# Attention on transposed scores, big-row loads, and a hand-written order of MM1, MM2 and attention

## The chip, the cores and the metric

The kernel runs on one core of one Trainium2 chip. The metric is device time in microseconds of one execution; three runs of the kernel before gave 509.43, 510.44 and 511.20 us, median 510.44. The engines are TensorE (PE for matmuls, PEld for weight loads in the profile), VectorE (DVE), ScalarE (ACT), GpSimd (POOL) and SyncE (SP), each with an instruction stream of its own.

## What is computed

The inputs q, k, v have the shape (batch 8, heads 8, sequence 576, head size 64), in f32. Heads 0 to 3 attend only to the last 32 positions, heads 4 to 7 only to earlier positions that are equal modulo 32:

```python
scores = scale * np.matmul(q, k.transpose(0, 1, 3, 2))
rel = pos[:, None] - pos[None, :]
mask_local = (rel >= 0) & (rel < stride)
mask_strided = (rel >= 0) & (pos[None, :] % stride == pos[:, None] % stride)
...
attn = np.exp(scores)
attn = attn / (np.sum(attn, axis=-1, keepdims=True) + 1e-09)
return np.matmul(attn, v).astype(np.float32)
```

The result, laid out as x of 4608 tokens by 512, goes through two dense layers: h = x @ w_in (512 by 2048), r = max(h, 0), out = (r * r) @ w_out (2048 by 512). The output is f32.

## The kernel before

Heads are worked on in pairs, so that a unit (a pair of one batch entry) has 128 rows of head size. The batch has 32 units, two local and two strided ones per batch entry. `attn_local_pair` loads q and k as 64 partitions by 9 rows and transposes each with nine 64-column transposes (L175), copies them out of the bank (L177), and takes the scores of six blocks of 96 queries by 128 keys (L201). `softmax_T` takes the exponential (L126), multiplies each block by a mask and sums its rows in the same instruction (L135), takes the reciprocal (L140) and builds a diagonal matrix of the reciprocals (L148). A matmul with that diagonal transposes and normalises the weights (L220), ScalarE copies them (L227), a matmul with v follows (L233), and VectorE writes the result into xt, the transposed x (L238). `attn_strided_pair` does the same on rows that are regrouped by residue modulo 32; each group of 7 residues is a block of 126, the last one of 72 (L264 to L336), and v comes in ten loads (L256).

xt has 4608 columns, cut into nine chunks of 512. For a chunk, MM1 has 16 output blocks of four matmuls each (L349), a relu on ScalarE (L353) and a square on VectorE (L354); MM2 has four row blocks of 16 matmuls each (L363), a copy on ScalarE (L367) and a store by SP (L368).

The order that the code is written in is attention by unit, with quarters of MM1 and whole MM2s between units (`drain_moe`). The framework then orders the instructions of each engine by a schedule of its own, and gives out the buffers. PSUM has eight banks: one for transposes, two for scores, two for the weights, one for the output of attention, one for MM1 (psh) and one for MM2 (psy). All loads go through POOL's queue, which also converts f32 to bf16.

## Time and profile before

| | |
|---|---|
| timed runs, median | 510.44 us |
| span of the profiled execution | 512.0 us |
| PE busy | 414.4 us, 81% |
| DVE busy | 281.4 us, 55% |
| POOL busy | 253.7 us, 50% |
| ACT busy | 196.8 us, 38% |
| packets on POOL's queue | 152896 |

The profiled execution's own time is its span: the profile shows nothing around it, and it lies 1.6 us above the median of the timed runs. Busy time of PE counts a matmul from its start to a modelled end, which lies after the start of the next one, so the price of a matmul is read from the distance of starts, and a wait shorter than that tail does not show as idle. An idle time names the engine and line that released it.

### The profile page before, as it was taken

The page shows a single profiled execution, that of the slowest core. Times are in us where ns is not written, and L with a number is a line of the kernel's source. Part 1 is how long each engine was busy: PE and PEld are TensorE (multiplying, and loading weights), DVE is VectorE, ACT ScalarE, POOL GpSimd, SP SyncE. Part 2 cuts the span into 40 slices and gives each one's busy share as a digit, 9 for nine tenths or more (in the row PEclk, how much of TensorE's full clock was granted, in tenths as well). Part 3 has the DMA queues.
Part 4 walks back from the last instruction along what each step waited for, and adds up shares of the span by engine and source line. Part 5 has one row for each costly group of instructions (what it writes and reads, how often), then busy time and mean ns, then how long its engine had stood idle before and what let it go on. Part 6 is the DMA issues. An engine that isn't in the chain of part 4 may idle for free.

```text
span 512.0 us, 8132 instructions
## 1 busy us (share of the span) xinstructions
PE 414.4 (81%) x2784; PEld 198.7 (39%) x2784; DVE 281.4 (55%) x1232; ACT 196.8 (38%) x437; POOL 253.7 (50%) x392
## 2 busy tenths in 40 slices
PE   1344489897999799879987998799889987779775
...
GB/s 36 197 139 98 69 59 63 91 88 64 41 31 103 70 39 54 92 108 49 41 66 69 31 35 66 70 31 32 57 42 1 2 42 42 0 1 61 20 22 61
DMA packets 158121, 29.23 MB, mean 57 GB/s; under 512 B 150912, under 2 KB 152960, under 8 KB 158080
## 3 DMA queue, kind: packets, MB, share of 16 engines
q0 software_dynamic: 152896, 19.27, 53.8%
...
## 4 chain that ended last, share of the span: by engine, by line
PE 65%; POOL 11%; DVE 9%; ACT 7%; issue 4%; DMA 3%; POOLq 0%; ACTq 0%
PE psh L349 29%; PE psy L363 22%; DVE xt L336 7%; ACT r_sb L353 6%; POOL svwb L256 3%; PE po L233 3%; PE po L322 2%; DMA w_in_b<-in_moe_w_in_dram 2%; PE psc L201 2%; PE pat L302 2%; PE pat L220 2%; PE ptr L175 1%; POOL w_out_b L114 1%; DVE e_m L135 1%; POOL vt L186 1%
## 5 line engine op out<-in xcount | busy, mean ns | idle before, releaser
L349 PE MATMUL psh<-xt,w_in_b 128*128 128x512 bf16 x576 | 171.8, 411 | 22.5 <-ACT r_sb L353 16.9
L363 PE MATMUL psy<-w_out_b,g_sb 128*128 128x512 bf16 x576 | 156.0, 389 | 3.2 <-ACT y_sb L367 2.3
L353 ACT ACTIVATE r_sb<-psh 128x512 bf16<-128x512 f32 x144 | 86.0, 597 | 148.0 <-PE psh L349 146.8
L256 POOL DMA_DIRECT2D svwb<-in_v_dram x160 | 99.9, 744 | 22.4 <-PE pat L302 15.2
L354 DVE TENSOR_TENSOR g_sb<-r_sb 128x512 bf16<-128x512 bf16 x144 | 60.3, 418 | 82.5 <-ACT r_sb L353 82.3
L349 PEld LDWEIGHTS <-w_in_b 128*128 128x128 bf16 x576 | 53.5, 102 | 78.9 <-issue 41.8
L363 PEld LDWEIGHTS <-g_sb 128*128 128x128 bf16 x576 | 55.7, 99 | 67.4 <-issue 9.0
L336 DVE CAST xt<-po 128x504 bf16<-128x504 f32 (+1 forms) x32 | 45.0, 1408 | 49.7 <-PE po L322 49.2
L126 ACT ACTIVATE e_sb<-psc 96x512 bf16<-96x512 f32 (+2 forms) x96 | 44.8, 517 | 37.3 <-PE psc L201 23.1
L367 ACT COPY y_sb<-psy 128x512 f32<-128x512 f32 x36 | 21.1, 586 | 94.3 <-PE psy L363 76.5
L148 DVE TENSOR_TENSOR diag<-ident,rinv 96x384 bf16<-96x384 bf16 (+2 forms) x96 | 50.4, 525 | 0.3
L135 DVE CUSTOM_DVE_ANT_0 e_m<-e_sb,mask_loc_g 96x128 bf16<-96x128 bf16 x192 | 46.4, 277 | 4.6 <-ACT e_sb L126 4.2
L135 DVE CUSTOM_DVE_ANT_0 e_m<-e_sb,mask_str 126x126 bf16<-126x126 bf16 (+1 forms) x160 | 36.1, 271 | 21.4 <-ACT e_sb L131 11.9
L322 PE MATMUL po<-sat_sb,svwb 126*64 126x126 bf16 (+1 forms) x160 | 16.4, 234 | 33.5 <-DVE xt L336 12.4
L168 POOL DMA_DIRECT2D kb<-in_k_dram x32 | 25.9, 812 | 25.3 <-PE ptr L175 18.5
L249 POOL DMA_DIRECT2D kb<-in_k_dram x32 | 27.4, 862 | 22.2 <-PE ptr L264 22.1
L166 POOL DMA_DIRECT2D qb<-in_q_dram x32 | 26.7, 850 | 19.4 <-PE ptr L175 17.7
L247 POOL DMA_DIRECT2D qb<-in_q_dram x32 | 27.5, 866 | 16.8 <-PE ptr L264 16.2
L186 POOL DMA_DIRECT2D vt<-in_v_dram x32 | 32.5, 1016 | 0.4 <-issue 0.2
L227 ACT CAST at_sb<-pat 128x384 bf16<-128x384 f32 (+1 forms) x64 | 25.0, 396 | 11.8 <-PE pat L220 11.2
L135 DVE DVE_READ_ACCUMULATOR2_ANT ssum<- 96x1 f32 (+2 forms) x352 | 28.5, 81 | 0.0
L322 PEld LDWEIGHTS <-svwb 126*64 126x64 bf16 (+1 forms) x160 | 10.0, 115 | 44.8 <-issue 17.9
...
## 6 DMA issues: line engine op xcount, KB each, us to landing
...
w_in_b<-in_moe_w_in_dram POOLq DMA_DIRECT2D x4, 512.0 KB, 8.9
...
svwb<-in_v_dram POOLq DMA_DIRECT2D x128, 15.8 KB, 2.3
...
```

Of the source, the lines that this page charges most:

```text
L126: nc.scalar.activation(e_sb[:, 0:gn, :], ps_sc[:, 0:gn, :], AF.Exp, scale=scale)
L135: nc.vector.tensor_tensor_reduce(out=e_m[0:w, t, 0:mask3[t].shape[-1]], in0=e_sb[0:w, t, 0:mask3[t].shape[-1]], in1=mask3[t], scale=1.0, s ...
L148: nc.vector.tensor_tensor(diag4[0:w, 0:gn, 0:w], id_b, rinv[0:w, 0:gn, :].to_broadcast([w, gn, w]), op=ALU.mult)
L186: nc.gpsimd.dma_start(out=vt[:, 1:6, hh, :], in_=win)
L247: nc.gpsimd.dma_start(out=qb[:, :, hh, :], in_=q[b, h0 + hh] .rearrange("(j p) d -> p j d", p=64))
L256: nc.gpsimd.dma_start(out=vwb[0:nt, hh, :], in_=src_v[7 * t:7 * t + nr, :, hh, :])
L322: nc.tensor.matmul(ps_ot[:, t, 0:nt], vrb[tt][0:nt, hh, :], ats[hh][0:nt, t, 0:nt], start=True, stop=True)
L336: nc.vector.tensor_copy(dst, src)
L349: nc.tensor.matmul(psh[:, 0:cw], w_in_b[:, kk, 128 * ff:128 * (ff + 1)], xt[kk][:, cols], start=(kk == 0), stop=(kk == 3))
L353: nc.scalar.activation(r_sb[:, 0:cw], psh[:, 0:cw], AF.Relu)
L354: nc.vector.tensor_tensor(g_sb[:, ff, 0:cw], r_sb[:, 0:cw], r_sb[:, 0:cw], op=ALU.mult)
L363: nc.tensor.matmul(psy, g_sb[:, ff, 128 * j:128 * (j + 1)], w_out_b[:, ff, :], start=(ff == 0), stop=(ff == 15))
```

## The change

The whole body is written anew, and `tc.manual_schedule()` makes each engine's order that of the code.

- Loads. q and k of local units come by SP in f32, 96 partitions with rows of six positions (L83), and POOL casts them (L98). Those of strided units come by POOL's queue, 72 partitions with rows of eight positions (L89). v has three loads per local unit and two per strided unit (L107 to L118). The order of residues in a strided unit is such that a block of 72 holds four residues.
- Scores are computed transposed, keys on partitions (L191), so the weights need no transpose before they meet v. The mask is one multiplication for 576 columns (L203, L206). v has a 65th column of ones, so the matmul with v gives the sums as well (L231); VectorE takes their reciprocal and normalises (L242, L243). The result is transposed back (L254) and copied into xt (L259, L261).
- Order. Attention of a batch entry is a list of 26 steps (`attn_steps`): T transposes q or k, S takes the scores, D the matmul with v, E writes xt. Batch entry 0 runs alone; then in phase ph MM1 of chunk ph and MM2 of chunk ph - 1 alternate in groups of four matmuls, and after each group the next due steps of batch entry ph + 1 are put. Exponentials, masks and squares are put some groups later (`later`, `tick`).
- Banks. MM1 has two banks (ps_h), MM2 one (ps_y), and all of attention shares five (ps_t).

```diff
-    ps_h = ctx.enter_context(tc.tile_pool(name="ps_h", bufs=1, space=bass.MemoryType.PSUM))
-    ps_y = ctx.enter_context(tc.tile_pool(name="ps_y", bufs=1, space=bass.MemoryType.PSUM))
...
+    ps_h = ctx.enter_context(tc.tile_pool(name="ps_h", bufs=2, space=PS))
+    ps_y = ctx.enter_context(tc.tile_pool(name="ps_y", bufs=1, space=PS))
+    ps_t = ctx.enter_context(tc.tile_pool(name="ps_t", bufs=5, space=PS))
+
+    ctx.enter_context(tc.manual_schedule())
...
+    ident = singles.tile([128, 128], BF16)
+    mask_loc = singles.tile([128, NL, QL], BF16)
+    mask_str = singles.tile([SP_, 1, SP_], BF16)
+    vls = [singles.tile([128, 2, NL, VP], BF16, name=f"vl{i}") for i in range(NV)]
+    vss = [singles.tile([SP_, NBS, VP], BF16, name=f"vs{i}") for i in range(NV)]
+    es = [singles.tile([128, 1280], BF16, name=f"e{i}") for i in range(3)]
+    xt = [singles.tile([128, T], BF16, name=f"xt{p}") for p in range(4)]
+    w_in_b = singles.tile([128, 4, d_ff], BF16)
+    w_out_b = singles.tile([128, 16, d_model], BF16)
...
+    def load_qk(u):
+        b, p = units[u]
+        s = st[u] = {}
+        for name, src in (("q", q), ("k", k)):
+            if is_local(u):
+                t = qk_st.tile([QL, 2, 6 * D], FP32, name=f"{name}_st")
+                nc.sync.dma_start(
+                    out=t,
+                    in_=src[b, 2 * p:2 * p + 2].rearrange("h (p j) d -> p h (j d)", j=6))
+                s[name + "f"] = t
+            else:
+                t = qk_in.tile([SP_, 2, NJ * D], BF16, name=f"{name}_s")
+                nc.gpsimd.dma_start(
+                    out=t,
+                    in_=src[b, 2 * p:2 * p + 2].rearrange("h (p j) d -> p h (j d)", j=NJ))
+                s[name] = t
...
+    def cast_qk(u):
+        s = st[u]
+        for name in "qk":
+            t = qk_in.tile([QL, 6, 2, D], BF16, name=f"{name}_l")
+            nc.gpsimd.tensor_copy(t.rearrange("p j h d -> p h j d"),
+                                  s[name + "f"].rearrange("p h (j d) -> p h j d", j=6))
+            s[name] = t
...
+            t = vls[n % NV]
+            nc.gpsimd.dma_start(
+                out=t[:, :, 0, 0:D],
+                in_=v[b, 2 * p:2 * p + 2, 0:128, :].rearrange("h p d -> p h d"))
+            for hh in range(2):
+                src = v[b, 2 * p + hh]
+                win = bass.AP(src.tensor, src.offset + 64 * D,
+                              [[D, 128], [QL * D, NL - 1], [1, D]])
+                nc.gpsimd.dma_start(out=t[:, hh, 1:NL, 0:D], in_=win)
...
+    clock = [0]
+    pending = []
+
+    def later(n, fn, key=None):
+        pending.append((clock[0] + n, key, fn))
+
+    def run_due(test):
+        due = [x for x in pending if test(x)]
+        for x in due:
+            pending.remove(x)
+        for x in sorted(due, key=lambda x: x[0]):
+            x[2]()
+
+    def tick():
+        clock[0] += 1
+        run_due(lambda x: x[0] <= clock[0])
...
+    def step_T(u, name):
+        s = st[u]
+        local = is_local(u)
+        n, w = (6, QL) if local else (NJ, SP_)
+        src = s[name]
+        src = src.rearrange("p j h d -> p (j h d)" if local else "p h c -> p (h c)")
+        pt = ps_t.tile([128, S], BF16, name="pt")
+        for j in range(n):
+            nc.tensor.transpose(pt[:, w * j:w * (j + 1)], src[:, 128 * j:128 * (j + 1)],
+                                ident[0:w, 0:w])
+        dst = qkT.tile([128, S], BF16, name=f"{name}T")
+        if local:
+            o = dst.rearrange("c (p j) -> c p j", j=6)
+            i = pt.rearrange("c (j p) -> c p j", j=6)
+        else:
+            o, i = dst, pt
+        if name == "q":
+            nc.scalar.copy(o, i)
+        else:
+            nc.vector.tensor_copy(o, i)
+        s[name + "T"] = dst
...
+    def blk_pos(h, j):
+        return NJ * (j % 2) + 4 * h + j // 2
...
+    def step_S(u):
+        s = st[u]
+        qT, kT = s["qT"], s["kT"]
+        local = is_local(u)
+        w, n = (QL, NL) if local else (SP_, NJ)
+        kn = 128 if local else SP_
+        hn = n // 2
+        e = es[u % 3]
+        s["e"] = e
+        banks = [[None, None], [None, None]]
+        for half in range(2):
+            for row in range(2):
+                banks[row][half] = ps_t.tile([128, 512], FP32, name="pt")
+            for i in range(hn):
+                t = half * hn + i
+                klo = w * t if not local else max(0, w * t - 32)
+                for row in range(2):
+                    rows = slice(64 * row, 64 * row + 64)
+                    nc.tensor.matmul(banks[row][half][0:kn, w * i:w * (i + 1)],
+                                     kT[rows, klo:klo + kn], qT[rows, w * t:w * (t + 1)],
+                                     start=True, stop=True)
+
+        def expo(row, half):
+            lo = S * row + S // 2 * half
+            nc.scalar.activation(e[0:kn, lo:lo + S // 2], banks[row][half][0:kn, 0:S // 2],
+                                 AF.Exp, scale=scale)
+
+        def masks(row):
+            if local:
+                x = e[:, S * row:S * (row + 1)]
+                nc.vector.tensor_tensor(x, x, mask_loc.rearrange("p t c -> p (t c)"), op=ALU.mult)
+            else:
+                x = e[0:kn, S * row:S * (row + 1)].rearrange("p (t c) -> p t c", c=w)
+                nc.vector.tensor_tensor(x, x, mask_str.to_broadcast([w, n, w]), op=ALU.mult)
+
+        expo(0, 0)
+        later(1, lambda: expo(0, 1), u)
+        later(2, lambda: (masks(0), expo(1, 0)), u)
+        later(3, lambda: expo(1, 1), u)
+        later(4, lambda: masks(1), u)
...
+    def step_D(u, part):
+        run_due(lambda x: x[1] == u)
+        s = st[u]
+        e, vt = s["e"], s["v"]
...
+            w, kn, tot = SP_, SP_, NBS
+            n0, n1 = ((0, 6), (6, 12), (12, 16))[part]
+            rhs = vt
+            pos = lambda n: SP_ * blk_pos(n % 2, n // 2)
+            src = lambda n: NJ * (n % 2) + n // 2
+        po = ps_t.tile([128, 6, D + 1], FP32, name="pt")
+        for n in range(n0, n1):
+            nc.tensor.matmul(po[:, n - n0, :], e[0:kn, pos(n):pos(n) + 128],
...
+        rinv = small.tile([128, 6, 1], FP32, name="rinv")
+        nc.vector.reciprocal(rinv[0:w, 0:m], po[0:w, 0:m, D:D + 1])
+        nc.vector.tensor_tensor(x, po[0:w, 0:m, 0:D],
+                                rinv[0:w, 0:m].to_broadcast([w, m, D]), op=ALU.mult)
...
+        px = ps_t.tile([128, S], BF16, name="pt")
+        for t in range(n):
+            nc.tensor.transpose(px[:, w * t:w * (t + 1)],
+                                x[:, 2 * t:2 * t + 2, :].rearrange("p h d -> p (h d)"),
+                                ident[0:w, 0:w])
+        dst = xt[p][:, b * S:(b + 1) * S]
+        if local:
+            nc.vector.tensor_copy(dst, px)
+        else:
+            nc.vector.tensor_copy(dst.rearrange("c (p j) -> c p j", j=NJ),
+                                  px.rearrange("c (j p) -> c p j", j=NJ))
...
+    def mm1(c, ff):
+        if ff == 0:
+            gs[c] = g_pool.tile([128, 16, 512], BF16, name="g_sb")
+        g = gs[c]
+        ph = ps_h.tile([128, 512], FP32, name="ph")
+        for kk in range(4):
+            nc.tensor.matmul(ph, w_in_b[:, kk, 128 * ff:128 * (ff + 1)],
+                             xt[kk][:, 512 * c:512 * (c + 1)], start=(kk == 0), stop=(kk == 3))
+        r = r_pool.tile([128, 512], BF16, name="r")
+        nc.scalar.activation(r, ph, AF.Relu)
+        later(1, lambda: nc.vector.tensor_tensor(g[:, ff, :], r, r, op=ALU.mult))
...
+    def mm2(c, i, pool=None):
+        j, part = divmod(i, 4)
+        g = gs[c]
+        if part == 0:
+            ys[c] = (pool or ps_y).tile([128, 512], FP32, name="py" if pool is None else "ph")
+        py = ys[c]
+        for ff in range(4 * part, 4 * part + 4):
+            nc.tensor.matmul(py, g[:, ff, 128 * j:128 * (j + 1)], w_out_b[:, ff, :],
+                             start=(ff == 0), stop=(ff == 15))
+        if part == 3:
+            y = y_pool.tile([128, 512], FP32, name="y")
+            nc.scalar.copy(y, py)
+            r0 = 512 * c + 128 * j
+            nc.sync.dma_start(out=out[r0:r0 + 128, :], in_=y)
...
+    def attn_steps(b):
+        u0 = 4 * b
+        T = lambda i, nm: (lambda: step_T(u0 + i, nm))
+        Sc = lambda i: (lambda: step_S(u0 + i))
+        Dd = lambda i, part: (lambda: step_D(u0 + i, part))
+        E = lambda i: (lambda: step_E(u0 + i))
+        order = [T(0, "q"), T(0, "k"), T(1, "q"), Sc(0), T(1, "k")]
+        for i in range(4):
+            order.append(Dd(i, 0))
+            if i + 1 < 4:
+                order.append(Sc(i + 1))
+            order.append(Dd(i, 1))
+            if not is_local(u0 + i):
+                order.append(Dd(i, 2))
+            if i + 2 < 4:
+                order += [T(i + 2, "q"), T(i + 2, "k")]
+            order.append(E(i))
+        return order
...
+    for i in range(4):
+        load_qk(i)
+    load_v(0)
+    load_v(1)
...
+    make_identity(nc, ident)
+    casts(0)
+    load_v(2)
+    load_v(3)
...
+    load_w_in(0)
...
+    for i in range(1, 4):
+        load_w_in(i)
+    loads(1)
+    for i in range(4):
+        load_w_out(i)
+    casts(1)
+
+    for fn in attn_steps(0):
+        fn()
+        tick()
+
+    NCH = T // 512
+    for ph in range(NCH + 1):
+        groups = []
+        if ph < NCH:
+            for ff in range(16):
+                groups.append(lambda ff=ff: mm1(ph, ff))
+                if ph > 0:
+                    groups.append(lambda i=ff: mm2(ph - 1, i))
+        else:
+            groups = [lambda i=i: mm2(ph - 1, i, ps_h) for i in range(16)]
+        steps = attn_steps(ph + 1) if ph + 1 < B else []
+        if ph + 2 < B:
+            loads(ph + 2)
+        if ph + 2 < B:
+            casts(ph + 2)
+        done = 0
+        for n, g in enumerate(groups):
+            g()
+            tick()
+            want = (n + 1) * len(steps) // len(groups)
+            while done < want:
+                steps[done]()
+                done += 1
```

On POOL's queue at the start of the program, before the change (qb, kb and vt are q, k and v of the first unit, w_in_b is MM1's weight):

```order
L76 AFFINE_SELECT mask_loc_g_104<-mask_loc_g_104 96x128
L96 AFFINE_SELECT mask_str<-mask_str 126x126
L166 DMA qb<-in_q_dram 64x9x64
L168 DMA kb<-in_k_dram 64x9x64
...
L181 DMA vt<-in_v_dram 128x64
L186 DMA vt<-in_v_dram 128x5x64
L110 DMA w_in_b<-in_moe_w_in_dram 128x2048 x4
L114 DMA w_out_b<-in_moe_w_out_dram 128x512 x3
```

After it (vl is v of local units, ident the identity, q_st and k_st the f32 rows that SP loaded):

```order
L89 DMA k_s<-in_k_dram 72x2x512
L107 DMA vl_96<-in_v_dram 128x2x64
L114 DMA vl_96<-in_v_dram 128x5x64 x2
L107 DMA vl_97<-in_v_dram 128x2x64
L114 DMA vl_97<-in_v_dram 128x5x64 x2
masks.py:197 MEMSET ident 128x128
masks.py:199 ISA
masks.py:199 AFFINE_SELECT ident<-ident 128x128
L98 CAST q_l<-q_st 96x2x6x64
L98 CAST k_l<-k_st 96x2x6x64
L98 CAST q_l<-q_st 96x2x6x64
L98 CAST k_l<-k_st 96x2x6x64
```

The masks stood ahead of all loads, and stand now behind the loads of all four units and the casts of two.

On TensorE in the middle of the program, before (psy is MM2's bank, psh MM1's, psc the scores' bank):

```order
L363 LDWEIGHTS g_sb
L363 MATMUL psy<-w_out_b,g_sb 128x512
L349 LDWEIGHTS w_in_b
L349 MATMUL psh<-xt_119,w_in_b 128x512
...
L349 MATMUL psh<-xt_122,w_in_b 128x512
L201 LDWEIGHTS qT_3186
L201 MATMUL psc<-kT_3187,qT_3186 96x128
```

After it, in phase 1 (ph is MM1's bank, py MM2's; the transposes of q are the first step of batch entry 2):

```order
L273 MATMUL ph<-xt_107,w_in_b 128x512
...
L273 MATMUL ph<-xt_110,w_in_b 128x512
L288 LDWEIGHTS g_sb
L288 MATMUL py<-w_out_b,g_sb 128x512
...
L156 LDWEIGHTS q_l
L156 MATMUL pt<-ident,q_l 128x96
```

A single matmul of MM2 stood ahead of four of MM1; now four of MM2 follow four of MM1, and a whole attention step follows.

On ScalarE in the middle of the program, before (r_sb is the relu's output, e_sb the exponential, at_sb the copied weights):

```order
L353 ACTIVATE r_sb<-psh 128x512 x2
L126 ACTIVATE e_sb<-psc 96x512 x2
L353 ACTIVATE r_sb<-psh 128x512
L126 ACTIVATE e_sb<-psc 96x256 x2
L353 ACTIVATE r_sb<-psh 128x512
L227 CAST at_sb<-pat 128x384 x2
L353 ACTIVATE r_sb<-psh 128x512
L227 CAST at_sb<-pat 128x192
L353 ACTIVATE r_sb<-psh 128x512
L227 CAST at_sb<-pat 128x192
```

After it (r is the relu's output, e_104 and e_105 the exponentials of two units, y the copy of MM2's output, qT the copy of the transposed q):

```order
L197 ACTIVATE e_104<-pt 128x288
L292 COPY y<-py 128x512
L197 ACTIVATE e_104<-pt 128x288
L276 ACTIVATE r<-ph 128x512
L197 ACTIVATE e_105<-pt 128x288 x2
L276 ACTIVATE r<-ph 128x512
L197 ACTIVATE e_105<-pt 128x288 x2
L165 COPY qT<-pt 128x576
```

The copies of the weights are gone, the exponentials stand singly or in twos between relus, and copies of q have come to ScalarE from VectorE.

## Rows read from the trace of the kernel before

**Rows 1.** the page: busy us, share of the span, instructions of each engine.
```profile
PE 414.4 (81%) x2784; PEld 198.7 (39%) x2784; DVE 281.4 (55%) x1232; ACT 196.8 (38%) x437; POOL 253.7 (50%) x392
```

**Rows 2.** busy us and instructions by stretch, granted clock, DMA share, GB/s.
```profile
0.00:64.00 64.00, 23.14 (x206) 16.32 (x206) 27.38 (x135) 13.72 (x33) 55.81 (x99) 1.00 1.08 108
64.00:416.00 352.00, 317.90 (x2255) 152.19 (x2256) 232.95 (x1035) 155.15 (x353) 197.85 (x294) 0.93 0.64 55
416.00:512.00 96.00, 73.33 (x325) 30.21 (x322) 21.06 (x63) 27.93 (x51) 0.00 (x0) 0.96 0.08 31
```

**Rows 3.** timeline, first unit: start us, us, engine, line, operation [idle before].
```profile
10.06 0.64 PE L175 MATMUL ptr<-ident,qb 64*128 64x64 bf16 x9 [10.06 <-DMA qb<-in_q_dram]
...
20.22 0.58 PE L349 MATMUL psh<-xt,w_in_b 128*128 128x512 bf16 x1 [0.46 <-DVE xt L238]
```

**Rows 4.** TensorE's timeline at full clock, 145 to 149 us.
```profile
145.42 0.44 PE L283 MATMUL psc<-kT,qT 64*126 64x126 bf16 x6
145.79 1.04 PE L349 MATMUL psh<-xt,w_in_b 128*128 128x512 bf16 x4
...
147.03 0.43 PE L264 MATMUL ptr<-ident,qb 64*128 64x64 bf16 x9
147.52 1.02 PE L349 MATMUL psh<-xt,w_in_b 128*128 128x512 bf16 x4
148.38 0.38 PE L363 MATMUL psy<-w_out_b,g_sb 128*128 128x512 bf16 x1
```

**Rows 5.** TensorE's timeline in the tail.
```profile
475.67 1.02 PE L349 MATMUL psh<-xt,w_in_b 128*128 128x512 bf16 x4 [0.47 <-ACT r_sb L353]
...
477.37 1.02 PE L349 MATMUL psh<-xt,w_in_b 128*128 128x512 bf16 x4 [0.47 <-ACT r_sb L353]
```

**Rows 6.** TensorE's waits: us in total, times, longest.
```profile
PE psh L349 <- ACT r_sb L353: 16.9, 39, 0.7
```

**Rows 7.** POOL's groups: shape, count, busy us, mean ns of one, idle before.
```profile
L186 POOL DMA_DIRECT2D vt<-in_v_dram x32 | 32.5, 1016 | 0.4 <-issue 0.2
...
L166 POOL DMA_DIRECT2D qb<-in_q_dram x32 | 26.7, 850 | 19.4 <-PE ptr L175 17.7 <-DMA w_in_b<-in_moe_w_in_dram 1.7
...
L63 POOL TENSOR_SCALAR_AFFINE_SELECT mask_loc_g<-mask_loc_g 96x512 bf16<-96x512 bf16 x1 | 0.6, 627 | 0.0
```

**Rows 8.** VectorE's groups by shape.
```profile
L354 DVE TENSOR_TENSOR g_sb<-r_sb 128x512 bf16<-128x512 bf16 x144 | 60.3, 418 | 82.5 <-ACT r_sb L353 82.3
...
L148 DVE TENSOR_TENSOR diag<-ident,rinv 96x384 bf16<-96x384 bf16 x32 | 17.5, 548 | 0.0
...
L266 DVE COPY kT<-ptr 128x576 bf16<-128x576 bf16 x16 | 13.4, 837 | 10.3 <-PE ptr L264 10.3
...
L177 DVE COPY kT<-ptr 128x576 bf16<-128x576 bf16 x16 | 7.3, 458 | 12.7 <-PE ptr L175 12.6
...
L140 DVE RECIPROCAL rinv<-ssum 126x4 f32<-126x4 f32 x32 | 5.6, 174 | 0.2
```

**Rows 9.** a dense stretch: all, line 349 alone, line 363 alone.
```profile
288.00:304.00 16.00, 15.92 (x129) 7.55 (x128) 11.30 (x56) 9.22 (x20) 4.43 (x6) 1.00 0.48 30
...
288.00:304.00 16.00, 8.92 (x33) 2.69 (x33) 1.00 0.48 30
...
288.00:304.00 16.00, 3.48 (x9) 0.87 (x9) 1.00 0.48 30
```

**Rows 10.** ScalarE's groups by shape.
```profile
L353 ACT ACTIVATE r_sb<-psh 128x512 bf16<-128x512 f32 x144 | 86.0, 597 | 148.0 <-PE psh L349 146.8
...
L126 ACT ACTIVATE e_sb<-psc 96x256 bf16<-96x256 f32 x32 | 10.5, 376 | 0.2
```

**Rows 11.** timeline, the span's end.
```profile
508.25 0.59 ACT L367 COPY y_sb<-psy 128x512 f32<-128x512 f32 x1 [3.75 <-PE psy L363]
```

**Rows 12.** TensorE's timeline after a long wait.
```profile
429.20 0.27 PE L322 MATMUL po<-sat_sb,svwb 72*64 72x72 bf16 x2 [2.26 <-DVE xt L336]
...
431.33 1.86 PE L349 MATMUL psh<-xt,w_in_b 128*128 128x512 bf16 x4 [0.69 <-ACT r_sb L353]
```

More of the change, by code (lines that the diff above doesn't have):

```diff
@@ L1 @@
-import dataclasses
 from contextlib import ExitStack
@@ L91 @@
-    nc.gpsimd.memset(mask_str, 1.0)
-    nc.gpsimd.affine_select(
-        out=mask_str, in_=mask_str, compare_op=ALU.is_ge, fill=0.0,
-        base=0, channel_multiplier=1, pattern=[[-18, 7], [-1, 18]],
-    )
-    nc.gpsimd.affine_select(
-        out=mask_str, in_=mask_str, compare_op=ALU.is_ge, fill=0.0,
-        base=17, channel_multiplier=-1, pattern=[[18, 7], [0, 18]],
-    )
-    xt = []
-    for p in range(4):
-        xt.append(singles.tile([128, T], BF16, name=f"xt{p}"))
+    NL = S // QL
@@ L357, in moe_mm2 @@
-    def moe_mm2(c):
-        cw = min(512, T - 512 * c)
-        g_sb = moe_state.pop(c)
-        for j in range(cw // 128):
-            psy = ps_y.tile([128, 512], FP32, name="psy")
-            for ff in range(16):
-                nc.tensor.matmul(
-                    psy, g_sb[:, ff, 128 * j:128 * (j + 1)],
-                    w_out_b[:, ff, :], start=(ff == 0), stop=(ff == 15))
-            y_sb = y_pool.tile([128, 512], FP32, name="y_sb")
-            nc.scalar.copy(y_sb, psy)
-            nc.sync.dma_start(out=out[512 * c + 128 * j:512 * c + 128 * (j + 1), :],
-                              in_=y_sb)
@@ L406, with is_local @@
-    while next_chunk < NCHUNK:
-        moe_chunk(next_chunk)
-        next_chunk += 1
-    drain_moe(10000)
+    w_in_v = moe_w_in.rearrange("(c p) f -> p c f", p=128)
+    w_out_v = moe_w_out.rearrange("(c p) f -> p c f", p=128)
+    units = [(b, p) for b in range(B) for p in range(H // 2)]
+    st = {}
+    def is_local(u):
+        return units[u][1] < H // 4
+    def load_qk(u):
[14 more added lines that the diff above has]
+                s[name] = t
@@ new lines, in cast_qk, with load_v @@
+    def cast_qk(u):
[5 more added lines that the diff above has]
+            s[name] = t
+    def load_v(u):
+        b, p = units[u]
+        n = (u // 4) * 2 + (p % 2)
+        if is_local(u):
+            t = vls[n % NV]
[7 more added lines that the diff above has]
+                nc.gpsimd.dma_start(out=t[:, hh, 1:NL, 0:D], in_=win)
+        else:
+            t = vss[n % NV]
+            for hh in range(2):
+                nc.gpsimd.dma_start(
+                    out=t[:, NJ * hh:NJ * (hh + 1), 0:D],
+                    in_=v[b, 2 * p + hh].rearrange("(p j) d -> p j d", j=NJ))
+        st[u]["v"] = t
@@ new lines, in load_w_in, with load_w_out @@
+    def load_w_in(i):
+        f = slice(512 * i, 512 * (i + 1))
+        nc.gpsimd.dma_start(out=w_in_b[:, :, f], in_=w_in_v[:, :, f])
+    def load_w_out(i):
+        c = slice(4 * i, 4 * (i + 1))
+        nc.gpsimd.dma_start(out=w_out_b[:, c, :], in_=w_out_v[:, c, :])
+    clock = [0]
[8 more added lines that the diff above has]
+            x[2]()
@@ new lines, in step_E @@
+    def step_E(u):
+        s = st[u]
+        b, p = units[u]
+        x = s["x"]
+        local = is_local(u)
+        n, w = (NL, QL) if local else (NJ, SP_)
+        px = ps_t.tile([128, S], BF16, name="pt")
[9 more added lines that the diff above has]
+                                  px.rearrange("c (j p) -> c p j", j=NJ))
+        st.pop(u)
@@ new lines, in loads, with casts @@
+    def loads(b):
+        for i in range(4):
+            load_qk(4 * b + i)
+            load_v(4 * b + i)
+    def casts(b):
+        for i in range(2):
+            cast_qk(4 * b + i)
+    for i in range(4):
+        load_qk(i)
+    load_v(0)
+    load_v(1)
+    nc.vector.memset(mask_loc, 1.0)
+    for t in vls:
+        nc.vector.memset(t[:, :, :, D:D + 1], 1.0)
+    for t in vss:
+        nc.vector.memset(t[:, :, D:D + 1], 1.0)
+    for e in es:
+        nc.vector.memset(e, 1.0)
+    make_identity(nc, ident)
@@ new lines @@
+    nc.vector.tensor_copy(mask_str.rearrange("p o (a h) -> p (o a) h", h=RH),
+                          res.to_broadcast([SP_, NA, RH]))
+    ms = mask_str[:, 0, :]
+    nc.gpsimd.affine_select(out=ms, in_=ms, compare_op=ALU.is_ge, fill=0.0,
+                            base=0, channel_multiplier=-1, pattern=[[1, SP_]])
+    for i in range(1, 4):
+        load_w_in(i)
+    loads(1)
+    for i in range(4):
+        load_w_out(i)
[3 more added lines that the diff above has]
+        tick()
@@ L413 @@
+    for _ in range(4):
+        tick()
 _INS = ['q', 'k', 'v', 'moe_w_in', 'moe_w_out']
```

362 lines of the change are left out of this document (47 added, 315 removed).

## The prediction

> **What bounds the kernel now.** I read the page first, then busy time by stretch, TensorE's timeline, and the groups by shape. TensorE is the busiest engine at 414.4 us of 512.0 [rows 1]; the next, VectorE, has 281.4, so a faster kernel must mean fewer idle or slow TensorE microseconds. Three stretches differ [rows 2]. In the first 64 us TensorE is busy for 23.1 us, while POOL (55.8 us) issues small loads; the first transposes start at 10.06 us, as soon as q lands [rows 3]. From 64 to 416 us it is busy for 318 of 352 us. From 416 to 512 us attention has run out, and it is busy for 73 of 96 us.
>
> How much of the busy time is work? At full clock a group of four 128x512 matmuls starts at 147.52 us and the next matmul at 148.38, so one costs 0.215 us [rows 4]; MM1 and MM2 have 144 + 144 groups of four = 1152, which is 248 us. Nine transposes take 147.03 to 147.52, 54 ns each; six score matmuls 145.42 to 145.79, 62 ns. The kernel has 2784 matmuls [rows 1], so 1632 small ones, at 55 ns, are some 90 us, and the whole is about 338 us. The other 174 us of the span are waits, part of them inside "busy", and low clock. The tail shows the commonest wait: psh has one bank, so four MM1 matmuls and one MM2 matmul (5 x 0.215 = 1.08) recur every 1.70 us, with 0.47 us idle behind the relu [rows 5]; over the run this wait is 16.9 us [rows 6].
>
> **The change, part by part.** The small TensorE work hardly shrinks: per local unit 12 + 12 + 12 + 6 = 42 matmuls, per strided unit 16 + 16 + 16 + 8 = 56, so 196 per batch and 1568 in all. What changes is their order, the banks (ph two, attention five in rotation) and the loads. So I sum by stages.
>
> *Until batch 0's attention ends.* POOL runs in order: ten loads come before the first cast, then four casts, four loads and the selects on the local mask. A load costs POOL about 0.85, a long v load 1.02 [rows 7]: 0.8 preamble + 4 x 0.85 + 2 x (0.85 + 2 x 1.02) + 0.5 for the identity = 10.5, then four casts. No row has a POOL cast; a select over 512 bf16 elements takes 0.63 [rows 7], so 768 take some 0.9 (0.63 if only fixed cost counts; twice, 1.9, if reading f32 does). Hence 14.2, then loads 3.4 and selects 1.8: the first mask multiply can run at 19.4 us. From there VectorE has per local unit, by the nearest rows [rows 8]: k copy 0.84, two masks at 0.45 (418 ns for 512 elements, scaled), two reciprocals 0.17, two normalisations 0.55 (diag's shape), final copy 0.46 = 3.6; per strided unit 4.2. With about 1.2 us of latency each, four units make 20.6: end at **40 us**. Bounds: 33 if VectorE alone counts, 52 at the old pace of 10 us for the first unit alone (10.06 to 20.22, where MM1 starts) [rows 3]. Batch 1's casts sit on POOL behind weights and loads, 19.4 + 2.6 + 12.9 + 2.6 + casts = about 39, no later.
>
> *Stage 0* (MM1 of chunk 0 beside batch 1): TensorE 64 x 0.215 + 196 x 0.055 = 24.6; VectorE 22.3; two attention steps stand between most groups, so a part of each chain is bare: **28** (24.6 to 37).
>
> *Stages 1 to 6*, which decide: 128 x 0.215 = 27.6, plus 196 small ones. I take 55 ns, by the bursts [rows 4]; the floor is 65 to 96 columns at the 0.42 ns a column of a big one, 33 ns for the mean of 77 columns and nothing else, and the ceiling is the whole dense stretch: 15.92 us hold 129 matmuls, 42 big, so (15.92 - 9.05)/87 = 79 ns with every hidden wait [rows 9]. That gives 10.8 (6.4 to 15.5), so 38.4. VectorE has 16 x 0.418 + 15.6 = 22.3 and ScalarE 16 relus at 0.597, 4 y copies at 0.59, 4 q copies at some 0.65 and 16 exponentials at 0.40 (0.376 for 256 elements [rows 10], plus 32 more) = 20.9, both covered by 38.4. POOL has 12.6 of loads and 3.6 of casts. Waits I add: the first D step of a batch reads 32 columns past row 0 of e, thus waits for the last mask, 0.6; at the stage's end MM1's fourth matmul waits for the last xt copy, 0.7; py's single bank 0.3. So **40** each, 240 in all (34.0 x 6 = 204 to 44.7 x 6 = 268).
>
> *Stages 7 and 8* have no attention: 2 x 27.7 = **55.4**. The relu is covered, since ph has two banks and four MM2 matmuls, 0.86 us, stand between MM1 groups. *MM2 of chunk 8*: 64 x 0.215 = **13.8**. *After the last matmul*: a 0.59 copy at 508.25 and the store until the span's end, **3.8** [rows 11], unchanged.
>
> Removed work counts only where it stood in a wait: the diag build, the masked sums, the slow xt copy, ScalarE's at copies. VectorE was not the bound, so none of these microseconds is subtracted; they are the reason why TensorE need not wait.
>
> Sum: 40 + 28 + 240 + 55.4 + 13.8 + 3.8 = **381 us** of span. The profiled execution took 512.0, 1.6 us over the median of the timed runs, so I forecast **379 us**.
>
> The Trainium skill, TensorE: Matmul & The Clock Gate, section "Back-to-back issue gap", speaks against my 55 ns: a stream of weight load and matmul pairs is said to sustain about 81 ns each at N=128. By that price a stage would have 15.9 us of small ones, and the sum would be about 417 us. The bursts of 54 and 62 ns at N=64 and 126 lie below it; the 79 ns of a dense stretch agrees, but that stretch has the relu wait in it.
>
> **The rivals.**
>
> *1. Small matmuls stay at 79 ns.* Speaks for it: the dense stretch's average [rows 9], and that after each semaphore wait a burst has to fill again. Against: there MM1 waits behind one bank; the new bursts are of 6 to 16. Time: 24 ns x 196 x 7 stages = 33 more, 412 us.
>
> *2. The in-order chain shows through.* Every step is placed by hand; if exps and mask (0.40 + 0.45 + 0.2) and reciprocal, normalisation and signalling before E (0.17 + 0.55 + 0.15) and part of the copies stay bare at each unit, that is 2.5 us x 4 = 10 a stage, 8.4 more than I have: 379 + 50 = 429 us. For it: in the middle stretch of today TensorE is 34 us short of busy although no engine is full [rows 2]. Against: four or more steps, some 5 us, lie between S and D except for a batch's first unit.
>
> *3. The clock falls and stays low: slower.* After 2.26 us of TensorE idle behind the xt copy, four matmuls took 1.86 us from first start to last end, against 1.02 at full clock [rows 4, 12]; one big matmul costs 0.21 us more, at 1.2 instead of 2.4 GHz. Mechanism: a short wait at every switch between a burst and a group of four. If all 1152 ran so, 379 + 242 = 621 us; it decides the sign once more than 131/0.21 = 624 of them, 54%, do. Against it: in the tail the engine idles 0.47 us in every 1.70 and still runs four in 1.02 [rows 5]. The mean granted clock now is 0.93 in the middle stretch [rows 2]. The skill's same page, section "A second HAM failure mode: psum-queue depth-cycling", names this mechanism, short idles while cycling through banks; the tail's rows do not bear it out here.
>
> *4. The change does not do what it says*, because POOL's in-order queue of casts and loads paces attention. It would need a cast of over 6 us to fill 38 us beside 12.6 of loads; the row next to it says 0.9. Counted with rival 2.
>
> **How the numbers follow.** Forecast 0.66 (355 to 400 us), rival 1 0.18 (400 to 422), rivals 2 and 4 0.11 (422 to 460), rival 3 0.04, and 0.01 for a tie by mishaps that I can't name. The unknown costs add to 33 + 25 + 204 + 73 = 335 at their floor and 52 + 37 + 268 + 73 = 430 at their ceiling. The range that leaves out 2 in 10 is 350 to 422. A measurement of this kernel tells about 0.3% from no change; faster by more has 0.95, within it 0.01, slower 0.04.
>
> **What would show it.** Right: in the middle of the new profile a stage recurs every 39 to 41 us, with TensorE idle under 2 us of it and granted clock 1.00; MM1's idle behind the relu, 16.9 us now, is nearly gone; the first big matmul starts at about 40 us; stages 7 and 8 take 27.7 each. Wrong: gaps over 0.3 us before L231, L254 or L191 in each batch (rival 2); a stage of 44 us without such gaps (rival 1); granted clock 0.5 in the middle (rival 3); L98 casts over 3 us, or L156 waiting for POOL (rival 4). If the first mask multiply waits for the selects past 25 us, the 40 us term fails.

## The result and the profile after

The changed kernel takes 378.93 us (377.17 to 379.63); beside it the kernel before took 510.0. The ratio is 0.7421 [0.7398, 0.7444]: faster by 131 us, and the forecast of 379 holds. It holds in part because errors of opposite sign cancelled. The profiled execution's span is 376.8 us. Times are medians of all runs of a kernel; the ratios leave out one slow run each of e8 (365.26 us) and e11 (356.62 us) below. The page of the changed kernel, engines and granted clock, beside [rows 1]:

```profile
PE 318.7 (85%) x2672; PEld 167.7 (45%) x2720; DVE 182.0 (48%) x446; ACT 166.2 (44%) x341; POOL 123.4 (33%) x163
...
PEclk9999999959999999999999999999999999999999
```

TensorE issues almost as many matmuls as before (2720 for 2784; the page lacks the records of 48) but is busy 96 us less: the busy time of before held waits, and stretches of low clock [rows 2]. The stages, from first MM1 to first MM1, with columns as in [rows 2]; the last row is stages 7, 8 and the last chunk's MM2:

```profile
78.65:117.95 39.30, 36.98 (x320) 19.18 (x326) 21.09 (x52) 19.06 (x40) 17.25 (x23) 0.93 0.61 71
117.95:155.00 37.05, 34.47 (x319) 18.33 (x327) 21.70 (x52) 19.06 (x40) 14.41 (x19) 1.00 0.64 96
...
303.32:373.00 69.68, 69.08 (x316) 31.22 (x322) 14.37 (x33) 25.55 (x44) 0.00 (x0) 1.00 0.12 46
```

A stage takes 37 us, 34.5 of them busy at full clock, where before 352 us held 318 busy ones at 0.93. Stage 1, the first row, is 2 us longer; its start ran at low clock. TensorE's timeline of the changed kernel, the start, stage 0 and two places of a later stage (they answer to [rows 3, 4]):

```profile
14.07 0.66 PE L156 MATMUL pt<-ident,q_l 96*128 96x96 bf16 x6 [14.07 <-POOL q_l L98]
...
21.98 0.65 PE L231 MATMUL pt<-vl,e 128*128 128x65 bf16 x6 [4.34 <-DVE e L203]
...
37.73 1.49 PE L273 MATMUL ph<-xt,w_in_b 128*128 128x512 bf16 x3 [0.22 <-DMA vl<-in_v_dram]
...
46.00 0.66 PE L156 MATMUL pt<-ident,q_l 96*128 96x96 bf16 x6 [6.79 <-POOL q_l L98]
...
54.10 0.57 PE L231 MATMUL pt<-vl,e 128*128 128x65 bf16 x6 [1.93 <-DVE e L203]
...
74.41 0.73 PE L231 MATMUL pt<-vs,e 72*128 72x65 bf16 x10 [1.45 <-DVE e L206]
...
157.09 0.42 PE L156 MATMUL pt<-ident,q_l 96*128 96x96 bf16 x6
157.35 1.03 PE L273 MATMUL ph<-xt,w_in_b 128*128 128x512 bf16 x4
...
163.77 0.32 PE L231 MATMUL pt<-vl,e 128*128 128x65 bf16 x5
165.53 0.20 PE L231 MATMUL pt<-vl,e 128*128 128x65 bf16 x1 [1.44 <-DVE e L203]
```

Three things stand here: six transposes in 0.26 us, 43 ns each; a hole of 6.79 us in stage 0; and a sixth weighted sum that waits 1.44 us once a batch, since its 128 columns reach into the second row's scores (e2 tests this). The waits of TensorE in the changed kernel (total, times, longest), where [rows 6] had 16.9 us behind the relu:

```profile
PE pt L156 <- POOL q_l L98: 20.9, 2, 14.1
PE pt L231 <- DVE e L203: 16.3, 10, 4.3
PE pt L254 <- DVE x_s L243: 7.4, 14, 1.1
PE pt L231 <- DVE e L206: 3.9, 4, 1.4
PE ph L273 <- DVE xt L261: 1.2, 6, 0.2
```

The wait behind the relu is gone. The hole comes from GpSimd's queue. Its timeline in the changed kernel:

```profile
36.79 0.70 POOL L89 DMA_DIRECT2D k_s<-in_k_dram  x1 [1.81 <-DMA w_in_b<-in_moe_w_in_dram]
...
42.06 3.06 POOL L129 DMA_DIRECT2D w_out_b<-in_moe_w_out_dram  x4
45.05 0.90 POOL L98 CAST q_l<-q_st 96x768 bf16<-96x768 f32 x1
```

Batch 1's casts stand behind loads whose issue waits for landings of earlier ones, and behind the output weights.

### The profile page after: what moved, and what is told of

It reads as the page before. It is cut to its first block, busy times and chain, and to the rows that moved or that the text cites. A ratio compares the mean times of both kernels' runs of the same rounds, so it can differ in the third digit from the quotient of the medians.

```text
span 376.8 us, 6791 instructions
## 1 busy us (share of the span) xinstructions
PE 318.7 (85%) x2672; PEld 167.7 (45%) x2720; DVE 182.0 (48%) x446; ACT 166.2 (44%) x341; POOL 123.4 (33%) x163
## 4 chain that ended last, share of the span: by engine, by line
PE 74%; DVE 7%; POOL 6%; DMA 5%; ACT 3%; issue 3%; POOLq 0%; ACTq 0%
PE ph L273 32%; PE py L288 27%; PE ph L288 4%; PE pt L156 4%; DMA w_in_b<-in_moe_w_in_dram 3%; PE pt L231 3%; PE pt L191 3%; ACT r L276 3%; DVE g_sb L277 2%; DMA q_s<-in_q_dram 2%; PE pt L254 2%; POOL vs L118 2%; DVE xt L261 1%; DVE x_s L243 1%; DVE e L203 1%
## 5 line engine op out<-in xcount | busy, mean ns | idle before, releaser
L273 PE MATMUL ph<-xt,w_in_b 128*128 128x512 bf16 x555 | 150.0, 388 | 2.6 <-DVE xt L261 1.2
L276 ACT ACTIVATE r<-ph 128x512 bf16<-128x512 f32 x144 | 86.0, 597 | 143.6 <-PE ph L273 141.8
L277 DVE TENSOR_TENSOR g_sb<-r 128x512 bf16<-128x512 bf16 x144 | 64.2, 446 | 145.4 <-ACT r L276 145.4
L288 PE MATMUL py<-w_out_b,g_sb 128*128 128x512 bf16 x486 | 129.0, 380 | 1.9 <-issue 0.9
L197 ACT ACTIVATE e<-pt 72x288 bf16<-72x288 f32 (+1 forms) x128 | 47.4, 407 | 9.5 <-PE pt L191 9.5
L231 PEld LDWEIGHTS <-e 72*128 72x128 bf16 (+1 forms) x448 | 25.8, 102 | 39.4 <-DVE e L203 17.8
L118 POOL DMA_DIRECT2D vs<-in_v_dram x32 | 25.9, 817 | 28.8 <-PE pt L231 26.0
L165 ACT COPY qT<-pt 128x576 bf16<-128x576 bf16 x32 | 20.4, 637 | 30.7 <-PE pt L156 30.7
L114 POOL DMA_DIRECT2D vl<-in_v_dram x32 | 28.3, 895 | 9.7 <-PE pt L231 4.0
L231 PE MATMUL pt<-vl,e 128*128 128x65 bf16 x192 | 13.4, 200 | 16.9 <-DVE e L203 16.3
L107 POOL DMA_DIRECT2D vl<-in_v_dram x16 | 11.9, 746 | 44.2 <-PE pt L231 43.2
L243 DVE TENSOR_TENSOR x_s<-pt,rinv 72x384 bf16<-72x384 f32 (+1 forms) x48 | 24.4, 509 | 1.7
L98 POOL CAST q_l<-q_st 96x768 bf16<-96x768 f32 x16 | 13.9, 869 | 21.0 <-DMA q_st<-in_q_dram 20.9
L231 PE MATMUL pt<-vs,e 72*128 72x65 bf16 x256 | 16.8, 202 | 4.2 <-DVE e L206 3.9
L242 DVE RECIPROCAL rinv<-pt 96x6 f32<-96x6 f32 (+2 forms) x80 | 14.7, 184 | 8.4 <-PE pt L231 8.2
L243 DVE TENSOR_TENSOR x_l<-pt,rinv 96x384 bf16<-96x384 f32 x32 | 17.7, 553 | 1.1
L203 DVE TENSOR_TENSOR e<-e,mask_loc 128x576 bf16<-128x576 bf16 x32 | 15.0, 475 | 5.8 <-POOL mask_loc L349 3.0
## 6 DMA issues: line engine op xcount, KB each, us to landing
w_in_b<-in_moe_w_in_dram POOLq DMA_DIRECT2D x4, 512.0 KB, 9.9
```

The costliest lines, as they stand in the source:

```text
L114: nc.gpsimd.dma_start(out=t[:, hh, 1:NL, 0:D], in_=win)
L118: nc.gpsimd.dma_start(out=t[:, NJ * hh:NJ * (hh + 1), 0:D], in_=v[b, 2 * p + hh].rearrange("(p j) d -> p j d", j=NJ))
L165: nc.scalar.copy(o, i)
L197: nc.scalar.activation(e[0:kn, lo:lo + S // 2], banks[row][half][0:kn, 0:S // 2], AF.Exp, scale=scale)
L231: nc.tensor.matmul(po[:, n - n0, :], e[0:kn, pos(n):pos(n) + 128], rhs[0:kn, src(n), 0:D + 1], start=True, stop=True)
L243: nc.vector.tensor_tensor(x, po[0:w, 0:m, 0:D], rinv[0:w, 0:m].to_broadcast([w, m, D]), op=ALU.mult)
```

## The experiments

All times are compared by the ratio to the kernel before on the same chip; a difference of 0.001 is 0.5 us. In kernels with the edit of e2, lines after 231 are one higher; in e4 they are one to two lower; in e11 the transposes are L161, the weighted sums L236 and MM2 L293.

**e1: batch 1's casts ahead of the output weights.** After `load_w_in(3)`:

```
-    loads(1)
-    for i in range(4): load_w_out(i)
-    casts(1)
+    load_qk(4); load_qk(5); casts(1)
+    load_v(4); load_v(5)
+    for i in range(6, 8): load_qk(i); load_v(i)
+    for i in range(4): load_w_out(i)
```

> The changed kernel, but batch entry 1's four casts stand on POOL right after MM1's weight loads, ahead of that entry's v and strided loads and of MM2's weights. Theory (the casts are late only because POOL works in order behind loads and weights): the hole of TensorE between 39.2 and 46.0 us closes, the first transposes of entry 1 run at about 38 us, and the time falls by 6.5 to 8.5 us, to 370 to 372. Rival (the loads that are pushed back 3.6 us become late in their place, or stage 0 is paced by VectorE so that an earlier start is waited away): within 2 us of 379.

Measured: 373.9 us, 0.73 [0.7269, 0.7332], 6 us less, a little under the theory's 6.5 to 8.5. The hole is closed (of the waits for L98's casts only the first, 13.7 us, remains), so its cause is shown. Part came back as a wait of 3.6 us for a mask. The timelines of VectorE and then GpSimd in e1 show where:

```profile
67.07 1.95 DVE L277 TENSOR_TENSOR g_sb<-r 128x512 bf16<-128x512 bf16 x1 [0.46 <-ACT r L276]
68.95 1.07 DVE L206 TENSOR_TENSOR e<-e,mask_str 72x576 bf16<-72x576 bf16 x1
...
67.15 0.82 POOL L98 CAST k_l<-k_st 96x768 bf16<-96x768 f32 x1
...
68.69 1.02 POOL L98 CAST k_l<-k_st 96x768 bf16<-96x768 f32 x1
```

A square that takes 0.43 us elsewhere takes 1.95, and a mask multiply 1.07 in place of 0.45, while GpSimd casts. e9 tests this.

**e2: 96-column weights for the last tile of a local unit.**

```
-            nc.tensor.matmul(po[:, n - n0, :], e[0:kn, pos(n):pos(n) + 128],
+            cw = w if is_local(u) and n == NL - 1 else 128
+            nc.tensor.matmul(po[0:cw, n - n0, :], e[0:kn, pos(n):pos(n) + cw],
```

> The changed kernel, but the last D matmul of each local row reads 96 columns of e as weights instead of 128, so that it no longer touches the next row's 32 columns. Theory (the first D of each batch entry waits for a mask that it needs only for those 32 columns): the waits of 1.3 to 1.9 us in front of the sixth matmul of L231, seven of them, go; time lower by 7 to 10 us, 369 to 372. Rival (the mask is needed one step later by the second D anyway, so the wait moves there): lower by under 3 us, 376 or more.

Measured: 368.67 us, 0.7207 [0.7172, 0.7243], 11 us less. The wait in e2, and a burst of six weighted sums:

```profile
PE pt L232 <- DVE e L203: 6.3, 2, 4.3
```

```profile
125.17 0.36 PE L232 MATMUL pt<-vl,e 128*128 128x65 bf16 x6
125.37 1.03 PE L274 MATMUL ph<-xt,w_in_b 128*128 128x512 bf16 x4
```

16.3 us in ten waits became 6.3 in two, and the gain is a little over the theory's 7 to 10: 32 columns that nobody reads cost a wait in nearly every batch.

**e3: such narrow weights for every weighted sum** (`cw = w`).

> As e2_row96, but all 448 D matmuls read weights of just their block's width, 96 or 72 columns instead of 128. Theory A (a small matmul costs only its streaming, some 30 ns, because a load of 128 columns is hidden and a narrower one is not): 15 to 25 ns more each, 7 to 11 us above e2_row96. Rival B (the width of the weights does not matter; the small price comes from few columns streamed and from no bank wait): within 1.5 us of e2_row96.

Measured: 372.52 us, 0.7269 [0.7235, 0.7303], 3 us above e2. The same burst in e3:

```profile
126.99 0.42 PE L232 MATMUL pt<-vl,e 128*96 128x65 bf16 x6
127.24 1.03 PE L274 MATMUL ph<-xt,w_in_b 128*128 128x512 bf16 x4
```

0.25 us for six, 42 ns each; e2 has 0.20, 33 ns. Only the 192 weighted sums of local units lose that much. The 256 of strided units, with weights of 72 columns now, take 0.21 us for six (150.31 to 150.52 us) where e2 has 0.19 (148.05 to 148.24). Together that is some 2.6 us (192 x 9 ns and 256 x 3.3 ns) of the 3 measured: the direction of theory A, at less than half of its 7 to 11 us.

**e7: the kernel before with two banks for MM1** (`ps_h` 1 to 2, `ps_at` 2 to 1). It asks whether the small matmuls of before really took 54 ns.

> The kernel before with one line changed twice: MM1's output has two banks, the transposed weights one instead of two. Theory (the commonest hidden wait of the kernel before is MM1's single bank, 1.70 us for five matmuls worth 1.08, and it also hides in the 54 and 62 ns that I read for small matmuls): the tail's 31 groups lose 0.6 us each, so at least 19 us less, 475 to 492, and bursts of transposes at full clock are followed by the next matmul after some 0.3 us for nine instead of 0.49. Rival (the bank that is taken from the weights costs as much, or the waits are elsewhere): 505 or more.

Measured: 500.85 us, 0.9785 [0.9745, 0.9824]: between theory and rival. The nine transposes of [rows 4] (L264) in e7, then eight of that line in the kernel before, ahead of a matmul of MM2, then a wait of e7:

```profile
146.56 0.43 PE L264 MATMUL ptr<-ident,qb 64*128 64x64 bf16 x9
146.93 0.39 PE L349 MATMUL psh<-xt,w_in_b 128*128 128x512 bf16 x1
```

```profile
151.95 0.40 PE L264 MATMUL ptr<-ident,kb 64*128 64x64 bf16 x8
152.29 0.39 PE L363 MATMUL psy<-w_out_b,g_sb 128*128 128x512 bf16 x1
```

```profile
PE po L322 <- DVE xt L336: 21.2, 16, 1.7
```

They take 0.37 us, 41 ns each, and the eight of before 0.34 us, 42 ns each: the 0.49 of [rows 4] held a wait for the relu, which the burst's own row does not show. The trace of before had the answer 5 us further on. The wait behind the relu is gone, yet its 17 us are not won: the waits for xt grew from 12.4 to 21.2 us and the granted clock of 64 to 416 us fell from 0.93 to 0.87. In the old order the bank, taken from attention, is worth 2%.

**e8: e1 and e2 together.**

> Both repairs together: batch 1's loads and casts queued ahead of the output weights, and 96-column weights for the last tile of each local unit's first product. Theory (they repair different waits, so they add): the ratios 0.730 and 0.7207 against 0.7421 of the plain change stand for 6 and 11 us, so 362 to 365 us where the kernel before takes 512. Rival (they overlap, since with early casts stage 0 waits for VectorE's masks anyway): 366 to 369, and the first-D wait of stage 0 stays at 3 us or more.

Measured: 361.42 us, 0.7059 [0.7019, 0.7099]. The sum of both gains stands at 0.7086, inside the interval: they add.

**e9: e8 with the casts on ScalarE** (`nc.scalar.copy` for `nc.gpsimd.tensor_copy` in line 98).

> As the kernel with both repairs, but the casts of q and k run on ScalarE instead of GpSimd. Theory (VectorE's instructions with two SBUF inputs slow down only while GpSimd casts): the squares of g, 0.42 us each and up to 1.95 while a cast ran, all stay under 0.8 us, the 3.6 us wait of stage 0 goes, and the time falls by 2 to 5 us against the kernel with both repairs. Rival 1 (the slow ones come from the loads that land then): squares of 1 us and more remain and the time is the same within 1 us. Rival 2 (ScalarE becomes late: four casts of about 0.8 us a stage stand ahead of a relu each): 2 to 6 us slower, as waits of TensorE for the relu or for q's copy.

Measured: 391.07 us, 0.7659 [0.7624, 0.7694], 31 us above e8. All squares of e9 (min/median/max), then waits of TensorE and ScalarE:

```profile
L278 DVE TENSOR_TENSOR g_sb<-r x144: 409/425/427, 41.0 to 372.0; 128x512 bf16<-128x512 bf16 x144
```

```profile
PE ph L274 <- ACT r L277: 21.3, 4, 5.7
...
ACT q_l L98 <- DMA q_st<-in_q_dram: 28.4, 11, 6.5
```

The theory of the slow squares is right: none is over 427 ns, where e8 has 1554 and e1 1950. The time is not: rival 2 has the place, waits for the relu, but neither the cause nor the size. It is not the casts' 0.83 us that costs, but that a cast, being in-order work, waits for its landing (28.4 us in all), and the relus behind it wait too, up to 5.7 us. The mean granted clock also fell, from 0.994 in e8 to 0.960; how the 31 us divide between waits and clock was not separated.

**e10: nothing interleaved.**

```
-            want = (n + 1) * len(steps) // len(groups)
-            while done < want: ...
+        for s in steps: s(); tick()      # after all groups of the stage
```

> The changed kernel with nothing interleaved: in each stage all MM1 and MM2 groups first, then all attention steps of the next batch. Theory (the gain is that matmul groups cover the attention's chain): a batch's attention alone takes what batch 0's took, about 23 us, in place of the 9 to 12 us that it adds to a stage now, so 11 to 14 us in each of 7 stages, and more if the clock drops in these stretches: 455 to 500 us. Rival (the shorter attention and the big-row loads are the gain, whatever the order): under 400 us.

Measured: 436.75 us, 0.8558 [0.8521, 0.8596], 58 us above the changed kernel: between theory and rival. One stage of e10, from its first MM1 over its first transposes to the next stage's MM1, and the busy times of the first part of its attention:

```profile
169.70 1.49 PE L273 MATMUL ph<-xt,w_in_b 128*128 128x512 bf16 x3 [0.22 <-issue]
...
198.69 0.42 PE L156 MATMUL pt<-ident,q_l 96*128 96x96 bf16 x6
...
217.78 1.49 PE L273 MATMUL ph<-xt,w_in_b 128*128 128x512 bf16 x3 [0.22 <-issue]
```

```profile
198.70:213.00 14.30, 10.16 (x171) 8.51 (x169) 10.82 (x28) 8.19 (x21) 7.47 (x10) 0.67 0.90 138
```

Attention alone takes 19.1 us, not batch 0's 23.7, of which 4.3 was the first wait for the mask. Interleaved it adds 37.0 - 27.6 = 9.4 us. The granted clock falls to 0.67 there, after waits of up to 1.2 us, and the big matmuls that follow begin at low clock too, so that they take 29.0 us for 27.6. Stages 1 to 6 take 48.0 us each (73.25 to 361.45 us), 10.6 more than interleaved, which is close to the theory's 11 to 14. Stage 0 takes 35.8 (37.50 to 73.25), 5.2 less: its transposes start behind the MM1 block, at 52.22, when batch 1's casts are done. So the theory's mechanism stands, and stage 0 is where its size was wrong.

**e5: one bank for MM1** (`ps_h` 2 to 1).

> The changed kernel with one bank for MM1's sums in place of two, the bank left unused. Theory A (four MM2 matmuls of 0.86 us between two MM1 groups cover a relu of 0.60): stages 1 to 8 are unchanged; stage 0, which has no MM2, and the last chunk's four copies of y pay up to 0.6 us each, so 3 to 10 us slower than the changed kernel: 382 to 389 us. Theory B (relus stand behind exponentials and q copies of 0.41 and 0.64 us on ScalarE and so end after the MM2 group): about one group in three waits 0.3 us in stages 1 to 7 as well: 390 to 400 us, with waits of ph for ScalarE over 15 us.

Measured: 384.14 us, 0.7533 [0.751, 0.7555], 6 us slower: theory A. Waits in e5:

```profile
PE ph L288 <- ACT y L292: 2.1, 3, 0.7
PE ph L273 <- ACT r L276: 2.1, 6, 0.5
```

**e6: 16 MM1 groups, then 16 MM2 groups.**

```
-                if ph > 0:
-                    groups.append(lambda i=ff: mm2(ph - 1, i))
+            if ph > 0:
+                for ff in range(16): groups.append(lambda i=ff: mm2(ph - 1, i))
```

> The changed kernel with all 16 MM1 groups of a stage first and then all 16 MM2 groups, attention steps spread over both as before. Theory A (the alternation hides y's single bank: a copy of 0.585 us and its release fall beside four MM1 matmuls): in the MM2 block every fourth group starts behind such a copy, four times a stage in 8 stages, 0.6 to 0.7 us each, about half of them behind an attention burst: 10 to 22 us slower than the changed kernel, with waits of py for ScalarE; MM1's two banks still hide the relus. Theory B (the two banks are what hides the relus and y's copy falls behind the bursts): within 4 us of the changed kernel. Theory C (relus bunch on ScalarE): waits of ph for ScalarE of 5 us and more.

Measured: 396.1 us, 0.7728 [0.7698, 0.7758], 16 us slower: theory A. A wait in e6:

```profile
PE py L288 <- ACT y L292: 10.6, 24, 0.7
```

No wait behind a relu, so not C; 10.6 of the 16 us are y's bank.

**e4: the changed kernel in the framework's order** (without `ctx.enter_context(tc.manual_schedule())`).

> The changed kernel with the hand order given up: the line that keeps the order as written is left out, so that the framework orders each engine's instructions. Its order differs in nearly every row, but from the third stage on it still puts four MM1, four MM2 and one attention burst in turn; in the first two stages it puts runs of scores and weighted sums of two units, single MM1 matmuls, and then 27 MM1 in a row. Theory A (what counts is that matmul groups and attention bursts alternate, not whose hand does it): stages 2 to 6 keep their 37 us, the first two lose some: 375 to 390 us. Theory B (the hand order is the gain): stages fall back towards the 47 to 50 us that each takes with the two parts kept apart: 420 us and more.

Measured: 351.44 us, 0.686 [0.6849, 0.687], 29 us faster than the hand order: the fastest of all, and neither theory saw it. Page, TensorE's three longest waits, and timeline of e4:

```profile
PE 318.5 (91%) x2720; PEld 166.8 (48%) x2720; DVE 184.4 (53%) x446; ACT 165.3 (47%) x341; POOL 124.7 (36%) x163
```

```profile
PE pt L155 <- POOL ident masks.py:199: 14.7, 1, 14.7
PE pt L230 <- DVE e L202: 4.9, 1, 4.9
PE pt L155 <- POOL q_l L97: 2.8, 1, 2.8
```

```profile
29.73 0.61 PE L272 MATMUL ph<-xt,w_in_b 128*128 128x512 bf16 x1 [1.41 <-DMA w_in_b<-in_moe_w_in_dram]
...
143.90 0.43 PE L190 MATMUL pt<-qT,kT 64*128 64x96 bf16 x12
...
147.12 0.34 PE L230 MATMUL pt<-vl,e 128*128 128x65 bf16 x6
```

ScalarE and VectorE of e4 between these two, then VectorE of the changed kernel, ahead of the sixth weighted sum at 165.53:

```profile
144.50 1.31 ACT L196 ACTIVATE e<-pt 128x288 bf16<-128x288 f32 x4
...
145.24 1.06 DVE L202 TENSOR_TENSOR e<-e,mask_loc 128x576 bf16<-128x576 bf16 x2 [0.18 <-ACT e L196]
```

```profile
165.03 0.44 DVE L203 TENSOR_TENSOR e<-e,mask_loc 128x576 bf16<-128x576 bf16 x1
```

TensorE is busy as long as by hand (318.7); only waits left. The first MM1 comes at 29.73 beside batch 0's attention, not at 37.73 behind it. On TensorE the first unit's scores stand as far ahead of its weighted sum as by hand: 3.2 us in both (143.90 to 147.12; 160.55 to 163.77). What differs is the order on the other two engines. Here the four exponentials follow each other, and both masks are done at 146.30, ahead of the weighted sum. By hand a relu and a copy of y stand between the exponentials, a square and a copy of k between the masks, and the second mask ends at 165.47, which left the 1.44 bare. From 80 us to 290 us TensorE has no idle time.

**e11: e4 with an earlier start.** Identity and masks first, batch 0's casts on other engines:

```
+            if u > 1: nc.gpsimd.tensor_copy(o, i)
+            elif name == "q": nc.scalar.copy(o, i)
+            else: nc.vector.tensor_copy(o, i)
...
+    load_qk(0); load_qk(1); make_identity(nc, ident)   # then the local mask
+    casts(0); load_v(0); load_v(1); load_qk(2); load_qk(3)
```

> The version in the framework's order, with the start rearranged: identity and local masks are built before any load that GpSimd issues, batch 0's casts of q and k run on ScalarE and VectorE as soon as their data lands, and the strided units' loads follow those of the first two units. In the framework's order TensorE waits 14.7 us for the first transpose, 4.9 for the first mask and 2.8 for batch 1's casts, 318.5 us are matmuls and 3.8 the end. Theory (the start is a chain of GpSimd, which waits on landed loads before it casts): the first transpose comes at 9 to 11 us, the first weighted sum follows 4 to 6 us behind it, and everything ends 5 to 9 us earlier: 343 to 347 us. Rival (MM1's weights, which land 24 to 37 us in, set when the first MM1 groups can run): TensorE waits for their landings instead and the time stays within 2 us of 351.

Measured: 353.65 us, 0.687 [0.6825, 0.6915]: no gain over e4. Waits in e11:

```profile
PE pt L161 <- POOL mask_loc L337: 4.9, 1, 4.9
PE py L293 <- DMA w_out_b<-in_moe_w_out_dram: 3.8, 2, 3.1
...
PE pt L236 <- DMA vl<-in_v_dram: 3.5, 2, 1.8
```

The first transpose comes 9.8 us earlier (4.9), the first MM1 only 0.6 (29.09): TensorE waits for landings instead, as the rival said, but above all of v and of the output weights rather than of MM1's. Which order of loads would win is open.

## Why the prediction was right, and where it was not

- *Attention of batch 0 until 40:* first MM1 at 37.73. The first mask multiply came at 21.46, not 19.4, because GpSimd waited for landings between its loads (1.93 and 1.47 us), which I had added up as pure issue time. The chain behind it took 16.3 us for my 20.6: no run shows the 1.2 us of latency that I gave each unit, and VectorE's own 15.6 us came close alone. (With these my lower bound should have read 35, not 33.) A cast took 0.87 us for my 0.9.
- *Stage 0, 28 us: failed.* It took 40.92 (37.73 to 78.65). The step that failed is that batch 1's casts come at "about 39, no later": they ran at 45.05. e1 shows that 6 of the 12.9 us hang on it. The stage is busy for 25.7 us, and beside the hole TensorE waits four times for masks, 5.7 us in all, and three times for normalised results, 2.5 us. These are the bare chains, for which I had put 3.4 us over the 24.6 of work.
- *Stages 1 to 6, 40 us each:* 37.4 on average (224.67 for 240). The step that failed is the price of 55 ns. A stage of 37.08 less 27.6 of big matmuls and 2.58 idle leaves 6.9 us for 196, 35 ns, near my floor of 33. My reading of [rows 4] held a hidden wait (e7). The wait of the first weighted sum, 0.6 in my sum, is 1.44 (e2); a wait of 0.5 for the last normalised result, ahead of L254, I had left out. The wait for the last xt copy took 0.2, not 0.7.
- *Rival 1* (79 ns) is refuted: bursts of 96 columns take 43 ns. The Trainium skill, TensorE: Matmul & The Clock Gate, section "Back-to-back issue gap", gives 81 ns at N=128. The changed kernel has no burst of 128 columns; in the kernel before, eight scores of 128 columns, over 64 rows, take 0.37 us (133.74 to 134.11 us), 46 ns each, so that this price is not borne out either.
- *Rival 2* is real in small: 1.4 + 0.5 us a stage, not 10. *Rival 3:* the clock stayed at 1.00 from stage 2 on. The record has it low only about the end of stage 0, 0.52 from 74.3 to 84.5 us, behind a wait of 1.45. Four matmuls at 46.47 us, behind the hole, took 1.91 us and so ran at low clock as well, though the record says 1.00 there. *Rival 4* was where stage 0 failed, through the queue and not through the cast's price.
- *Stages 7, 8 and the last MM2:* 69.68 for 69.2; the end 3.8 for 3.8. The two banks do what I said, but e5 shows them worth only 6 us in this order: four MM2 matmuls cover most relus by themselves.
- The sum, 376.8 for 381: -2.3 + 12.9 - 15.3 + 0.5. With stage 0's error alone the span would have been 394; the time was right by cancelling, the range by its width. The last step, 1.6 us off the span, went the wrong way: each run here takes 1.7 to 1.8 us more than its span (378.49 for 376.8), so that a span of 381 meant 383 us, and 3 us of the hit on 379 are luck of another kind.
- Where the 131 us came from: keeping groups and bursts apart gives back 58 (e10). The other 74, a difference and no measurement of its own, belong to the shorter attention, the loads and the banks together; a second bank for MM1, taken from attention, gave 11 in the old order (e7). A part of the 131 goes through the clock: its mean over the profiled span rose from 0.946 to 0.986. By my estimate from these two and the spans that is at most 22 us (0.054 x 512.0 less 0.014 x 376.8), since it counts waits as well. How the rest divides was not tried.
